# Turning the thresholded weights: TensorE takes row tiles 1 and 3 of the first eight head pairs, and the instruction order is planned anew

## The chip, the cores and the metric

The kernel runs on one core of one Trainium2 chip. The metric is the device time of the whole kernel in microseconds. Before the change it is 623.7 us, the median of three runs (623.29 to 623.73). The profiled run took 623.28 us, of which the profile covers a span of 621.5 us from the first to the last instruction, so a span and a time of this kernel differ by 1.8 to 2.2 us.

## What is computed

```python
scores = (q @ k.T) / 8                       # 8 batches, 8 heads, 576 x 576, head size 64
thresh = scores.max(-1) - tau                # tau = 0.02
attn   = exp(where(scores >= thresh, scores, -1e9) - scores.max(-1))
x      = (attn / (attn.sum(-1) + 1e-9)) @ v  # heads side by side: 8 x 576 x 512
u      = x + (x.T @ U @ V).T                 # rank 32, along the sequence
out    = u + relu(u @ w_ch1) @ w_ch2         # 512 -> 2048 -> 512
```

## The kernel before

**Pairs and row tiles.** The work is cut into 32 pairs of heads, four pairs to a batch. A pair's 576 rows are nine half tiles of 64, handled as row tiles 0 to 3 of 128 rows and a tile 4 that two neighbouring pairs share. So two pairs make nine score blocks, and the kernel has 144 of them. I number the blocks from 0, in the order in which TensorE runs them. Batch 0 is blocks 0 to 17, batch 1 blocks 18 to 35.

**One score block.** TensorE writes the scores of both heads into two PSUM tiles (`scores`, L449). VectorE reads each of them once, scaled and negated, to SBUF and takes the row minimum on the way (`weigh`, L462). There is one such pair of PSUM tiles only, so block n+1 can't start before both reads of block n are done. ScalarE makes the threshold (L475) and the exponentials (L482). VectorE selects and sums (`select`, L489) into a bf16 tile of the ring `w_ring`, which holds four blocks.

**Turning.** The product with `v` (`product`, L582, for the first four pairs L586) contracts over the columns, so the selected weights have to be turned. There are two ways. `turn_w` (L502) is a DMA transpose that SyncE issues, for one head or for both at once. `turn_pe` (L509) is five TensorE transposes into a PSUM bank, after which ScalarE copies the bank to SBUF (`copy_w`, L519). Before the change, the first eight pairs (`EARLY = 8`) turn row tiles 1, 2 and 3 of head 1 on TensorE and of head 0 by one-head transfers; row tile 0 and the shared tile go by two-head transfers. Head 0 of row tile 3 of pair 3 goes to TensorE too. All later pairs use two-head transfers only.

**What follows a pair.** The products are scaled by the inverse sums (`make`, L607, or for later pairs `low_part`, `join`, `norm`), then come `narrow` (L635), the low-rank products `low_rank` (L643) and `spread` (L658, and `spread4`, L695, once a batch), the sum `sum_u` (L665), `narrow_u` (L672) and a turn by TensorE, `turn_u` (L680), copied by `copy_u` (L686). When all four pairs of a batch are through, the mixer of that batch may run: 16 `up` groups of four matmuls (L750) with a relu on ScalarE each (L740), and `down` groups of four (L783), four to an output tile. The row tile 4 of two batches is done together: `rest` (L766).

**The order.** A planner in the kernel, the class `Order`, decides the order of every engine's instructions when the kernel is built. It holds a list of tasks with a cost and dependencies, keeps a clock for each engine, and takes from the tasks that can start within `PATIENCE` of the earliest the one with the lowest rank, which is the time when it became ready plus an offset by kind and phase from the table `OFF`. Mixer tasks have a due step, counted in score blocks (`DUE`); before it they are taken only when nothing else can start. Where the planner sees TensorE idle it puts filler matmuls on a zero tile (`fill`, L293). [...]

**Buffers that matter below.** Four PSUM banks for all that isn't scores, two `wT_ring` buffers for the turned weights (pair p needs the products of pair p-2 to be done), two `qkraw` buffers, and GpSimd's queue for the loads of q, k and the mixer's weights (`W1_AT` and `W2_AT` name the block whose read opens each weight load).

## Time and profile before

| | busy us | share of the 621.5 us span |
|---|---|---|
| TensorE matmul | 604.8 | 97% |
| VectorE | 521.5 | 84% |
| ScalarE | 479.3 | 77% |
| GpSimd | 285.5 | 46% |

A matmul is recorded from its start until its modelled end, so records of neighbours overlap. The spacing from one start to the next is what a matmul costs. The page's second part cuts the span into 40 slices of 15.5 us and prints the busy share of each in tenths. The timeline lists instructions in order of time, with equal neighbours merged into one row: start, length, engine, line, operation, tiles, count, and, in brackets, how long the engine was idle before and what ended that.

The program has 73 fillers and 25 turns by TensorE (125 matmuls of L509). The span has 127 DMA transposes into `wT_ring` and 16 into `wT4`.

### The profile page before, as it was taken

The page shows a single profiled execution, that of the slowest core. Times are in us where ns is not written, and L with a number is a line of the kernel's source. Part 1 is how long each engine was busy: PE and PEld are TensorE (multiplying, and loading weights), DVE is VectorE, ACT ScalarE, POOL GpSimd, SP SyncE. Part 2 cuts the span into 40 slices and gives each one's busy share as a digit, 9 for nine tenths or more (in the row PEclk, how much of TensorE's full clock was granted, in tenths as well). Part 3 has the DMA queues.
Part 4 walks back from the last instruction along what each step waited for, and adds up shares of the span by engine and source line. Part 5 has one row for each costly group of instructions (what it writes and reads, how often), then busy time and mean ns, then how long its engine had stood idle before and what let it go on. Part 6 is the DMA issues. An engine that isn't in the chain of part 4 may idle for free.

```text
span 621.5 us, 16829 instructions
## 1 busy us (share of the span) xinstructions
PE 604.8 (97%) x6286; PEld 353.2 (57%) x6374; DVE 521.5 (84%) x1406; ACT 479.3 (77%) x983; POOL 285.5 (46%) x396
## 2 busy tenths in 40 slices
PE   8989999999999999999999999999999999999996
PEld 4556555565665655555656555555656555555543
DVE  5999998799888999899988999899999898993202
ACT  5779899978898767987898976897798867893540
POOL 8965456545455544535455554444565513211000
PEclk9999999999999999999999999999999999999999
DMA  7999999876976988889979898989998676653303
GB/s 161 172 169 175 154 141 170 137 134 129 171 141 121 169 156 163 140 145 167 161 142 148 135 163 151 150 134 177 162 135 170 141 124 118 117 93 60 69 1 84
DMA packets 205105, 86.27 MB, mean 139 GB/s; under 512 B 183136, under 2 KB 195376, under 8 KB 205024
## 3 DMA queue, kind: packets, MB, share of 16 engines
q1 hardware_dynamic: 190096, 62.23, 62.2%
q0 software_dynamic: 14048, 22.76, 18.7%
q8 instruction: 50, 0.82, 0.6%
q10 hardware_dynamic: 880, 0.21, 0.2%
q14 instruction: 31, 0.25, 0.2%
HBM read 36.86 MB, written 9.44 MB: 74 GB/s over the span
## 4 chain that ended last, share of the span: by engine, by line
PE 85%; DVE 8%; issue 3%; ACT 1%; DMA 1%; SPq 1%; DVEq 0%; ACTq 0%
PE scores L449 23%; PE bank L783 20%; PE bank L750 17%; PE bank L582 12%; PE bank L383 4%; DVE w_ring L489 3%; DVE s_sb L462 3%; PE bank L766 2%; PE bank L643 1%; PE bank L658 1%; PE bank L680 1%; PE bank L396 1%; DMA vraw_ring<-in_v_dram 1%; PE bank L509 1%; ACT e_sb L482 1%
## 5 line engine op out<-in xcount | busy, mean ns | idle before, releaser
L489 DVE SCALAR_TENSOR_TENSOR w_ring<-s_sb,thr,e_sb 128x576 bf16<-128x576 f32 x288 | 238.4, 846 | 10.2 <-ACT thr L475 5.2
L482 ACT ACTIVATE e_sb<-s_sb,m 128x576 bf16<-128x576 f32 x288 | 217.2, 770 | 27.2 <-DVE s_sb L462 26.1
L462 DVE TENSOR_SCALAR_CACHE_REDUCE s_sb<-scores 128x576 f32<-128x576 f32 x288 | 207.9, 751 | 30.9 <-PE scores L449 27.6
L449 PE MATMUL scores<-qkT 64*64 64x288 f32 x2304 | 178.8, 415 | 1.1 <-DVE s_sb L462 1.0
L630 POOL TENSOR_TENSOR x<-x,rec 128x256 f32<-128x256 f32 (+1 forms) x84 | 58.9, 702 | 169.3 <-DVE x L623 108.2
L783 PE MATMUL bank<-W2b,R 128*128 128x512 bf16 x541 | 133.3, 379 | 2.4 <-issue 0.6
L750 PE MATMUL bank<-uT,W1b 128*128 128x512 bf16 x470 | 120.0, 379 | 2.5 <-issue 0.5
L449 PEld LDWEIGHTS scores<-qkT 64*64 64x64 f32 x2304 | 78.0, 132 | 74.6 <-issue 17.8
L740 ACT ACTIVATE R<-bank 128x512 bf16<-128x512 f32 x144 | 84.5, 594 | 22.4 <-PE bank L750 14.5
L329 POOL DMA_DIRECT2D qkraw<-in_q_dram x125 | 81.9, 661 | 33.2 <-PE bank L383 26.9
L415 POOL TENSOR_TENSOR vh<-vraw_ring,vh 128x640 bf16<-128x640 f32 x32 | 50.6, 1581 | 78.8 <-ACT vh L411 69.2
L783 PEld LDWEIGHTS <-R 128*128 128x128 bf16 x576 | 53.3, 98 | 56.3 <-issue 5.7
L329 POOL DMA_DIRECT2D qkraw<-in_k_dram x125 | 81.2, 656 | 3.8 <-DMA qkraw<-in_q_dram 2.3
L750 PEld LDWEIGHTS <-W1b 128*128 128x128 bf16 x512 | 46.0, 98 | 52.1 <-issue 10.2
L582 PEld LDWEIGHTS <-wT_ring 128*128 128x128 bf16 x1120 | 64.8, 98 | 12.7 <-issue 8.8
L582 PE MATMUL bank<-vh,wT_ring 128*128 128x128 bf16 x1120 | 71.9, 219 | 0.0
L794 DVE TENSOR_TENSOR o<-bank,x 128x512 f32<-128x512 f32 x36 | 24.4, 683 | 39.7 <-PE bank L783 36.7
L475 ACT ACTIVATE thr<-m,tau_t 128x2 f32<-128x2 f32 x144 | 42.2, 293 | 4.6 <-DVE s_sb L462 4.2
L389 ACT COPY qkT<-bank 128x512 f32<-128x512 f32 x64 | 35.5, 584 | 9.5 <-PE bank L383 9.1
L623 DVE TENSOR_TENSOR x<-bank,x 128x256 f32<-128x256 f32 (+1 forms) x84 | 30.7, 375 | 8.1 <-ACT x L619 7.3
L383 PE MATMUL bank<-ident,qkraw 128*128 128x128 f32 x256 | 34.9, 275 | 1.0 <-DMA qkraw<-in_q_dram 0.3
L619 ACT COPY x<-bank 128x256 f32<-128x256 f32 (+1 forms) x84 | 26.7, 329 | 10.6 <-PE bank L582 9.9
(70 smaller groups left out, 498.2 us busy)
## 6 DMA issues: line engine op xcount, KB each, us to landing
out_dram<-o SPq DMA_DIRECT2D x72, 128.0 KB, 2.5
vraw_ring<-in_v_dram SPq DMA_DIRECT2D x32, 160.0 KB, 3.7
qkraw<-in_k_dram POOLq DMA_DIRECT2D x63, 80.0 KB, 4.8
qkraw<-in_q_dram POOLq DMA_DIRECT2D x62, 80.0 KB, 3.9
vraw_ring<-in_v_dram SPq DMA_DIRECT2D x32, 128.0 KB, 4.3
qkraw<-in_q_dram POOLq DMA_DIRECT2D x63, 64.0 KB, 4.1
qkraw<-in_k_dram POOLq DMA_DIRECT2D x62, 64.0 KB, 4.4
W1b<-in_moe_w_ch_dram POOLq DMA_DIRECT2D x8, 256.0 KB, 5.5
```

What stands on the lines that cost most here:

```text
L329: queue.dma_start(pr.qkraw[part, to, j, :], src[:, j, of, :])
L383: nc.tensor.transpose(bank[t.got[0]][:, i * P:(i + 1) * P], pr.qkraw[:, t0 + i, :, :], ident)
L415: nc.gpsimd.tensor_tensor(out=pr.vh[:, :, :, 1, :], in0=pr.vraw.rearrange("p j t d -> p t j d"), in1=pr.vh[:, :, :, 0, :], op=ALU.subtract)
L449: nc.tensor.matmul(pair_bank[j][part, c, 0:HC], a.tT[hs, 0, rows], a.tT[hs, 1, cs], start=True, stop=True)
L462: nc.vector.tensor_scalar(out=s_sb.rearrange("p (a c) -> p a c", a=2), in0=pair_bank[x][:, :, 0:HC], scalar1=-scale, scalar2=None, op0=ALU ...
L482: nc.scalar.activation(out=e_sb, in_=s_sb, func=ACT.Exp, bias=m[:, x:x + 1], scale=-1.0)
L489: nc.vector.scalar_tensor_tensor(out=w_sb[:, 0:S], in0=s_sb, scalar=thr_[:, x:x + 1], in1=e_sb, op0=ALU.is_le, op1=ALU.mult, accum_out=pr. ...
L582: nc.tensor.matmul(av[:, 2 * a + j, :], w, pr.vh[:, kt, j, :, :], start=first, stop=last_)
L630: nc.gpsimd.tensor_tensor(out=x, in0=x, in1=over_sum(part), op=ALU.mult)
L740: nc.scalar.activation(out=R2[:, fts, lo:hi], in_=bank[t.got[0]].rearrange("p (f c) -> p f c", c=hi - lo), func=ACT.Relu)
L750: nc.tensor.matmul(bank[t.got[0]], W1b[:, dt, ft * P:(ft + 1) * P], bt.uT[:, dt, :], start=(dt == 0), stop=(dt == 3))
L783: nc.tensor.matmul(ch, R2[:, ft, lo:lo + P], W2b[:, ft, :], start=(ft == 0), stop=(ft == 15))
```

## The change

In the first eight pairs, row tiles 1 and 3 of both heads are now turned by TensorE, and row tiles 0 and 2 by one transfer for both heads. This leaves no one-head transfer: 23 of them go, 8 two-head transfers and 7 turns by TensorE are added. At the same time the planner gets new numbers: the offsets `OFF`, the patience of GpSimd and SyncE, the landing times of transfers, the issue cost of a two-head transpose (1.9 to 1.4), and the due steps of weights and mixers. Two dependencies are added for the planner: a product waits until the output rows that it leads to are free (`opens`), and the first `down` of a tile waits for the one of the tile before (`got("down")`). What is computed stays the same. It is meant to relieve the DMA queue in the crowded opening and to fit the order to that.

```diff
-BOTH = 1.9
-W1_AT = (5, 7, 9, 11, 13, 15, 17, 19)
-W2_AT = (21, 22, 24, 25, 26, 27, 29, 30)
-DUE = (30, 48, 99, 104, 159, 168, 132, 156)
+W1_AT = (0, 3, 6, 8, 11, 14, 17, 19)
+W2_AT = (20, 21, 23, 24, 25, 26, 28, 29)
+DUE = (30, 48, 66, 84, 162, 120, 128, 156)
...
-    PATIENCE = (0, 0.2, 0.1, 0.55, 0)
+    PATIENCE = (0, 0.2, 0.1, 1.1, 1.35)
...
-    LANDING = (2.3, 1.8)
+    LANDING = (2.0, 1.4)
...
-        "down": (0, 0, 0), "exponential": (21, 43, -10.5), "finish": (-2, -4, -1),
+        "down": (0, 0, 0), "exponential": (27.75, 43, -10.5), "finish": (-2, 13, -1),
...
-        "turn_pe": (-25, 13, -1), "turn_rest": (-3, -2, -2), "turn_u": (-23, -6, -3),
+        "turn_pe": (-20.25, 13, -1), "turn_rest": (-5, -37.25, -6.25), "turn_u": (-36, -6, -3),
...
-            both = not (p < EARLY and 1 <= i < 4)
+            both = not (p < EARLY and i in (1, 3))
...
-            if i < 4 and (x == 1 and p < EARLY and i >= 1 or p == NPAIR - 1 and i == 3):
+            if i < 4 and (p < EARLY and i in (1, 3)):
...
-                    SP, BOTH, turn_w, [first_sel, sel] + free, dma=2.2)
+                    SP, 1.4, turn_w, [first_sel, sel] + free, dma=2.2)
...
-                done["wTs", p, g] + [done["vlo", p], got("AV", p - 1, g)], banks=1, kind="AV")
+                done["wTs", p, g] + [done["vlo", p], got("AV", p - 1, g)] + opens, banks=1, kind="AV")
...
-                    when=due + 38.75 * ft / 16)
+                    when=due + 35.75 * ft / 16)
...
-                        kind="p1", when=due + -11.75 + 9.75 * g)
+                        kind="p1", when=due + -0.75 + 10 * g)
...
-                when = due + 124 if i == 4 and b < B - 1 else due + 20.5 + 0.25 * (i + g / 4) / 4
-                halves.append(add(PE, 0.865, down, (relus4 if i == 4 else relus) + weights2 + halves,
-                                  banks=int(not g), kind="ch", when=when))
+                when = due + 133.5 if i == 4 and b < B - 1 else due + 48.5 + 14.25 * (i + g / 4) / 4
+                halves.append(add(PE, 0.865, down, (relus4 if i == 4 else relus) + weights2 + (
+                    halves or [got("down")]), banks=int(not g), kind="ch", when=when))
+            done["down"] = halves[0]
```

## The prediction

> **What bounds the kernel now.** I read the page's second part first, then the windows by stage, then the timelines of TensorE and VectorE around the stage borders.

> ```profile
> PE   8989999999999999999999999999999999999996
> DVE  5999998799888999899988999899999898993202
> ACT  5779899978898767987898976897798867893540
> ```

> TensorE looks full nearly everywhere, but its record has overlapping ends, so I don't trust the digit. The windows show a difference of stage.

> ```profile
> 12.00:83.00 71.00, 65.79 (x942) 40.55 (x941) 69.64 (x188) 57.48 (x115) 47.28 (x70) 1.00 1.13 163
> 83.00:91.00 8.00, 7.95 (x92) 5.39 (x88) 7.75 (x22) 7.02 (x15) 4.53 (x7) 1.00 1.17 210
> 91.00:557.00 466.00, 461.32 (x4825) 270.91 (x4896) 424.88 (x1146) 387.33 (x805) 220.43 (x297) 1.00 0.84 145
> 557.00:617.00 60.00, 59.40 (x387) 31.61 (x390) 14.04 (x31) 22.45 (x43) 3.21 (x5) 1.00 0.26 54
> ```

> The columns are window, length, busy time of TensorE matmuls, weight loads, VectorE, ScalarE and GpSimd, then clock, DMA share, GB/s. From 12 to 83 us VectorE is busy for 69.64 of 71 us: it is the bound, and TensorE has room (67 of the 73 fillers lie before block 23). From 91 us on VectorE has about 9% to spare and TensorE none.

> To find the border I added up the TensorE work in program order at the spacing that the timeline shows between starts: 1.13 us for a score block and 0.095 us for entering it, 0.863 for four `up` or `down` matmuls, 1.12 for twenty products (1.16 in the first four pairs), 0.87 for the eight turns of q and k and 0.14 for the ninth, 0.285 for a turn of weights, 0.28, 0.235 and 0.225 for `low_rank`, `spread` and `turn_u`, 0.056 for a matmul of `rest`, 0.216 for a filler or `spread4`. The clock minus this sum is lost time. It is 3.8 us at the end of block 0, 9.3 at block 12, 16.34 at block 22 (end 83.13 us), 17.29 at block 24 (90.77 us), 17.44 at block 25, and then hardly grows: 19.56 at block 143 (557.05 us). So from block 24 to the end TensorE runs without a gap, and everything that it holds is time. The border:

> ```profile
> 82.00 1.69 PE L449 MATMUL scores<-qkT 64*64 64x288 f32 x16
> ...
> 85.63 1.49 PE L449 MATMUL scores<-qkT 64*64 64x288 f32 x16
> 87.06 0.40 PE L680 MATMUL bank<-identb,ub 128*128 128x128 bf16 x4
> 87.29 1.28 PE L582 MATMUL bank<-vh,wT_ring 128*128 128x128 bf16 x20
> 88.41 1.03 PE L750 MATMUL bank<-uT,W1b 128*128 128x512 bf16 x3
> ```

> The block at 82.00 is number 22; the first `up` comes after block 23. The last 64 `down` start at 602.79 us, end at about 616.6, and the last addition and store take the remaining 4.9 us.

> [...] the records here do overlap, hence the sum over spacings. [...] the select is stuck behind the subtraction of GpSimd that began just before it and takes 1.93 us where 0.8 is usual.

> ```profile
> 36.95 1.40 POOL L415 TENSOR_TENSOR vh<-vraw_ring,vh 128x640 bf16<-128x640 f32 x1 [3.04 <-ACT vh L411]
> 37.04 1.93 DVE L489 SCALAR_TENSOR_TENSOR w_ring<-s_sb,thr,e_sb 128x576 bf16<-128x576 f32 x1
> ```

> **The change part by part.** *Turns on TensorE.* 7 x 5 = 35 matmuls are added. In the changed program 20 of them (90 against 70) come before the end of block 22, where TensorE is not the bound: no cost, hidden behind VectorE. The other 15 (70 against 55) are three turns on the path: 3 x 0.285 = 0.86 us.

> *Fillers.* 67 instead of 73, but 57 instead of 67 before block 22 ends and 10 instead of 6 after it: 4 x 0.216 = 0.86 us more on the path. (The ten: one ahead of block 23, six ahead of 31, three ahead of 42, none before the last `down`, where the old order has three.)

> *Work moved ahead of the border.* One `spread` (0.235) and one `spread4` (0.216) now come before block 22: 0.45 us less after it. The counts of all other TensorE work after block 22 are equal. So after block 22 the new order has 0.86 + 0.86 - 0.45 = 1.27 us more.

> *An earlier border.* The first `up` moves from after block 23 to before it. Between the ends of blocks 22 and 23 the new order holds 4.66 us of TensorE work, the old one 2.97 (with 3.63 on the clock). So TensorE is the bound from block 22 on instead of 24, and the 17.29 - 16.34 = 0.95 us that the old order loses between those blocks is gone. Net: +0.3 us for the same date of block 22.

> *The date of block 22.* It is VectorE's. Up to the two reads of block 21, which release block 22, both VectorE lists hold exactly the same instructions (the sums at 0.68 a read, 0.74 a select are equal), so the date moves only by stalls. Downward: of the 71 us, 1.4 are idle and some 3 us are selects stretched by GpSimd (1.93 and 1.83 us twice, 1.28, 1.20, 1.19); at best 2 us of this goes. Upward: ScalarE. Seven copies at 0.58 us spacing (0.69 as recorded) are 4.1 us more, and they fall here: at the exponentials of block 22 its list holds 68.7 us instead of 63.4, at a spacing of 0.68 an exponential. From block 10 to 21 it holds 36.7 us against 36.6 of VectorE work; before, it was 32.4. ScalarE becomes a second bound there, with no more than VectorE's own stalls to spare. I take +0.2 us, bounds -2 and +2.5.

> *The chain into the first `up`.* Between `low_rank` and `spread` of pair 3 the old order has two turns and the score matmuls of block 22, 1.6 us, the new one only one turn of 0.285 us, in which ScalarE's copy (0.26 us as recorded, plus two signals and its queue) can't fit. Likewise between `turn_u` and `up` there is 0.65 us (four turns of q or k and a filler) instead of 1.12 us of products, for a copy of 0.58 us. What waits behind these on TensorE is block 23 and all after it. The trace has no such wait; the nearest, products behind a copy at 35.28 us, idled 0.66 us. I take 0.3 us, bounds 0 and 1.5.

> *DMA.* 23 one-head transfers go and 8 two-head ones come: 15 issues fewer, at 1.2 to 1.4 us of SyncE each. No TensorE time after block 24 waits for a transfer now, so nothing is gained after the border; before it VectorE hides it. Products still come 2 to 3 blocks or more after their last select (1.5 in a few cases, all with a last tile turned by TensorE), so I cost this at nothing.

> *The steady part and the end.* New due steps change which mixer work fills a block, not how much there is. The new `opens` holds back the products of batch 7: pairs 28 and 29 run after block 139 instead of 131 to 138. Nine transposes then follow in a row; the last product has about 28 us of TensorE work between, enough for nine at 2.4 us (the spacing of four in 9.80 us at 553 us). I take 0, upper bound 2 us. The last group and the 4.9 us after it are alike.

> Sum: 0.3 + 0.2 + 0.3 = +0.8 us: 623.7 + 0.8 = 624.5 us.

> **Rivals.**
> *Slower: ScalarE and the tight chains.* The 4.1 us on ScalarE hold up selects before block 22, waits in front of `spread` and `up` open, the batched transposes make the end late. For it: 36.7 against 36.6 us[...]. Against it: ScalarE is busy only 57.48 of the 71 us now. With half of each upper bound (1.2 + 0.8 + 1.0) less the 0.5 already taken: about +2.5 on 624.5, so 627.0 us.
> *Faster: fewer collisions.* GpSimd's subtractions and casts fall between selects, VectorE starts block 22 up to 2 us earlier and the chains hold. 623.7 + 0.3 - 2.0 = 622.0 us. For it: five stretched selects. Against it: there are as many subtractions as before, and where they fall is chance. The transposes by DMA can't be the gain, since nothing on the path waits for them.
> *No change because the copies are hidden* is the forecast itself.

> **How the numbers follow.** Forecast, near no change: 0.42, 624.5 us. Slower rival: 0.36, 627.0. Faster rival: 0.22, 622.0. 0.2% is 1.25 us, so no change is 622.45 to 624.95. The forecast lies near its upper edge, so 0.05 of it goes to slower. Faster 0.22, same 0.37, slower 0.41. Range: from the faster rival less 1 us for gains that I don't see, 621.0, up to 623.7 + 0.3 + two thirds of the upper bounds of 2.5, 1.5 and 2 us, 628.0.

> **What would show it.** Right: 32 turns and 67 fillers, block 22 still ending near 83 us, VectorE full up to it, TensorE without a gap from block 22 on, and the rest from there as long as before within a microsecond. ScalarE as bound: idle time of L489 behind L482 before 83 us. The chains: idle time ahead of L658 or L750 near 85 us. The end: idle TensorE near 560 us. It is wrong if the lost time after block 24 grows by more than 2 us or block 22 moves by more than 2 us.

## The result and the profile after

The changed kernel takes 632.7 us, the median of four runs (631.9 to 634.0). Its ratio to the kernel before is 1.0135, with a 95% interval of 1.0096 to 1.0174: some 8 to 9 us slower. A ratio here is an estimate over the executions and not the quotient of the two medians, and it leaves out executions that are over 1.5% above the fastest of their kernel. The profiled execution took 634.0 us with a span of 632.2 us, so it shows 10.7 us more than the span of before; I account for that one.

The second part of the page:

```profile
PE   8889899999999999999999999999999999999997
DVE  5989998799998899899997999899998899785101
ACT  5669789988799867897889876897788865596530
PEclk9989899999999999999999999999999999999999
```

TensorE's granted clock falls twice in the first five slices; in the kernel before this row is 9 throughout. The windows by stage, cut where the same work ends in the new trace (block 22, the border, block 143), with the columns as before:

```profile
12.00:88.30 76.30, 69.11 (x968) 43.20 (x963) 70.07 (x189) 59.55 (x119) 48.64 (x70) 0.96 0.94 150
88.30:97.40 9.10, 9.10 (x96) 5.53 (x92) 7.70 (x20) 8.80 (x19) 6.80 (x10) 1.00 0.81 163
97.40:567.30 469.90, 467.34 (x4886) 270.01 (x4882) 424.99 (x1141) 384.62 (x798) 220.91 (x293) 1.00 0.82 142
567.30:628.00 60.70, 60.23 (x419) 32.52 (x411) 16.42 (x36) 26.23 (x51) 3.21 (x6) 1.00 0.28 53
```

The opening is 5.3 us longer up to block 22, but VectorE's busy time in it hardly grew (70.07 us against 69.64): VectorE now waits for 6 us there. The clock minus the sum of TensorE work, the measure of the prediction, shows where the 10.7 us lie. (All times in the table are counted from the first score block at the same date; the prices are those of the prediction to within 0.2 us in the sum.)

| up to the end of | before, us | lost | after, us | lost |
|---|---|---|---|---|
| block 6 | 27.2 | 5.0 | 27.9 | 6.4 |
| block 8 | 33.7 | 6.1 | 38.1 | 10.7 |
| block 15 | 56.9 | 11.4 | 60.4 | 15.4 |
| block 17 | 64.3 | 12.3 | 71.0 | 19.8 |
| block 22 | 83.3 | 16.5 | 88.6 | 22.4 |
| block 37 | 142.8 | 17.4 | 150.1 | 22.5 |
| block 42 | 161.4 | 17.5 | 171.7 | 25.3 |
| block 120 | 466.3 | 18.9 | 471.8 | 26.8 |
| block 121 | 470.8 | 18.8 | 476.7 | 28.6 |
| block 143 | 556.7 | 19.2 | 567.5 | 29.4 |

So the new order loses 5.9 us more up to block 22. After it it loses 7.0 us where the old one loses 2.7, in pieces: 2.8 between blocks 37 and 42, 1.8 at block 121, 0.6 each near blocks 82 and 132. From block 143 on both take the same time. In the opening, the view of TensorE's waits (columns: who waited for whom, us in total, times, longest) names two long ones. First after, from 10 to 90 us:

```profile
PE bank L585 <- DMA wT_ring<-w_ring: 2.3, 1, 2.3
PE scores L448 <- DVE s_sb L461: 2.2, 1, 2.2
PE bank L679 <- ACT wT_ring L518: 0.9, 1, 0.9
```

The same view of before has no wait over 0.7 us and none for a transposing transfer:

```profile
PE bank L509 <- DVE w_ring L489: 1.3, 3, 0.6
PE scores L449 <- DVE s_sb L462: 1.0, 2, 0.7
PE bank L586 <- ACT wT_ring L519: 0.7, 1, 0.7
```

**The first wait.** TensorE's timeline of after (lines of kernel.py are one lower than before):

```profile
28.06 0.66 PE L382 MATMUL bank<-ident,qkraw 128*128 128x128 f32 x4
31.05 1.34 PE L585 MATMUL bank<-vh,wT_ring 128*128 128x64 bf16 x40 [2.33 <-DMA wT_ring<-w_ring]
32.22 0.31 PE L395 MATMUL bank<-ident,qkraw 128*128 128x128 f32 x1
32.46 2.16 PE L448 MATMUL scores<-qkT 64*64 64x288 f32 x16
34.55 1.11 PE L382 MATMUL bank<-ident,qkraw 128*128 128x128 f32 x4
```

The product of pair 0, row tiles 2 and 3, waits for the two-head transfer of row tile 2. The view of its tile from 20 to 26 us has that one transfer, issued at 22.0 us, and its landing, 9.0 us after the issue:

```profile
L501 SPq DMA_TRANSPOSE wT_ring<-w_ring x1: 2009/2009/2009, 22.0 to 22.0; - x1
DMA to landing us min/median/max: 9.0/9.0/9.0
```

The scores of block 7 (the expectations below call it block 8), queued behind it, then take 2.16 us where 1.2 is usual, and four turns 1.11 instead of 0.66. The windows cut at the trace's own clock records say why: the window with the wait in it has only 1.51 us of TensorE, and the next 3.41 us run at half the clock.

```profile
29.15:32.56 3.41, 1.51 (x45) 1.40 (x49) 1.62 (x7) 1.12 (x3) 2.13 (x4) 1.00 0.96 160
32.56:35.97 3.41, 3.41 (x22) 1.76 (x23) 2.36 (x6) 1.21 (x3) 2.74 (x5) 0.50 1.28 149
```

**The second wait.** The full timeline of after, a collision of VectorE's select and GpSimd's subtraction:

```profile
61.52 2.48 DVE L488 SCALAR_TENSOR_TENSOR w_ring<-s_sb,thr,e_sb 128x576 bf16<-128x576 f32 x1
...
61.97 1.41 POOL L414 TENSOR_TENSOR vh<-vraw_ring,vh 128x640 bf16<-128x640 f32 x1
...
64.14 0.76 DVE L461 TENSOR_SCALAR_CACHE_REDUCE s_sb<-scores 128x576 f32<-128x576 f32 x1
...
64.96 0.47 PE L448 MATMUL scores<-qkT 64*64 64x288 f32 x4 [2.21 <-DVE s_sb L461]
```

The select is recorded from 61.52 us, before the subtraction, but ends only 0.6 us after it. The dates alone don't show that it waited for the subtraction; e9 below, which cuts only that, does (0.92 us instead of 2.48). The read of block 15 behind it is late, block 16 waits 2.21 us, and again 3.41 us of half clock follow:

```profile
63.28:66.69 3.41, 1.73 (x15) 0.80 (x16) 2.96 (x9) 1.75 (x4) 0.60 (x2) 1.00 0.61 90
66.69:70.10 3.41, 3.41 (x47) 2.69 (x49) 2.99 (x9) 2.51 (x5) 0.00 (x0) 0.50 0.82 160
```

### The profile page after: what moved, and what is told of

The parts are those of the page before. It is cut to its first block, busy times and chain, and to the rows that moved or that the text cites. A ratio compares the mean times of both kernels' runs of the same rounds, so it can differ in the third digit from the quotient of the medians.

```text
span 632.2 us, 16962 instructions
## 1 busy us (share of the span) xinstructions
PE 615.1 (97%) x6403; PEld 355.6 (56%) x6403; DVE 524.1 (83%) x1406; ACT 483.8 (77%) x990; POOL 289.1 (46%) x396
## 4 chain that ended last, share of the span: by engine, by line
PE 85%; DVE 5%; DMA 4%; ACT 2%; issue 2%; POOL 1%; SPq 1%; DVEq 0%; POOLq 0%; ACTq 0%
PE scores L448 22%; PE bank L782 19%; PE bank L749 17%; PE bank L581 12%; PE bank L382 4%; DMA wT_ring<-w_ring 3%; DVE w_ring L488 2%; PE bank L765 2%; DVE s_sb L461 2%; PE bank L642 1%; DMA vraw_ring<-in_v_dram 1%; PE bank L679 1%; PE bank L395 1%; PE bank L585 1%; PE bank L657 1%
## 5 line engine op out<-in xcount | busy, mean ns | idle before, releaser
L481 ACT ACTIVATE e_sb<-s_sb,m 128x576 bf16<-128x576 f32 x288 | 217.2, 770 | 38.0 <-DVE s_sb L461 37.3
L448 PE MATMUL scores<-qkT 64*64 64x288 f32 x2304 | 181.4, 417 | 2.4 <-DVE s_sb L461 2.4
L629 POOL TENSOR_TENSOR x<-x,rec 128x256 f32<-128x256 f32 (+1 forms) x84 | 61.2, 730 | 166.7 <-DVE x L622 113.3
L782 PE MATMUL bank<-W2b,R 128*128 128x512 bf16 x576 | 137.4, 379 | 0.0
L749 PE MATMUL bank<-uT,W1b 128*128 128x512 bf16 x512 | 123.7, 379 | 0.0
L739 ACT ACTIVATE R<-bank 128x512 bf16<-128x512 f32 x144 | 85.1, 595 | 20.8 <-PE bank L749 16.5
L581 PEld LDWEIGHTS <-wT_ring 128*128 128x128 bf16 x1120 | 64.0, 98 | 14.8 <-issue 11.4
L388 ACT COPY qkT<-bank 128x512 f32<-128x512 f32 x64 | 35.6, 584 | 10.2 <-PE bank L382 10.0
L382 PEld LDWEIGHTS bank<-ident,qkraw 128*128 128x128 f32 x256 | 29.4, 142 | 5.3 <-issue 2.5
```

The costliest lines, as they stand in the source:

```text
L382: nc.tensor.transpose(bank[t.got[0]][:, i * P:(i + 1) * P], pr.qkraw[:, t0 + i, :, :], ident)
L448: nc.tensor.matmul(pair_bank[j][part, c, 0:HC], a.tT[hs, 0, rows], a.tT[hs, 1, cs], start=True, stop=True)
L481: nc.scalar.activation(out=e_sb, in_=s_sb, func=ACT.Exp, bias=m[:, x:x + 1], scale=-1.0)
L581: nc.tensor.matmul(av[:, 2 * a + j, :], w, pr.vh[:, kt, j, :, :], start=first, stop=last_)
L629: nc.gpsimd.tensor_tensor(out=x, in0=x, in1=over_sum(part), op=ALU.mult)
L739: nc.scalar.activation(out=R2[:, fts, lo:hi], in_=bank[t.got[0]].rearrange("p (f c) -> p f c", c=hi - lo), func=ACT.Relu)
```

## The experiments

The ratios below are to the kernel before, run on the same chip, with 95% intervals. "The order kept" means that the planner's list is written down before anything is emitted (`plan`) and only the named entries of it are moved or added; numbers are positions of tasks in the list.

| run | median us | ratio |
|---|---|---|
| changed kernel | 632.7 | 1.0135 [1.0096, 1.0174] |
| e1 turning rule alone | 632.2 | 1.0130 [1.0086, 1.0174] |
| e2 new numbers alone | 631.9 | 1.0131 [1.0108, 1.0153] |
| e8 old kernel, one landing time moved 3% | 632.1 | 1.0123 [1.0079, 1.0167] |
| e3 nine fillers in the wait | 630.6 | 1.0108 [1.0087, 1.0128] |
| e4 product later | 630.6 | 1.0108 [1.0085, 1.0131] |
| e5 weights later | 629.2 | 1.0086 [1.0061, 1.0111] |
| e9 subtraction cut in five | 628.2 | 1.0067 [1.0044, 1.0089] |
| e18 weights later and cut | 625.6 | 1.0030 [1.0008, 1.0052] |
| e11 weights later, cut, nine fillers | 629.2 | 1.0083 [1.0051, 1.0115] |
| e16 changed, 19 fillers more | 632.0 | 1.0141 [1.0121, 1.0160] |
| e6 changed, no subtraction | 623.9 | 0.9997 [0.9966, 1.0028] |
| e7 before, no subtraction | 619.9 | 0.9944 [0.9922, 0.9966] |
| e12 e8 without subtraction | 623.5 | 0.9989 [0.9969, 1.0010] |
| e10 before, cut | 628.0 | 1.0051 [1.0025, 1.0076] |
| e13 before, 35 fillers fewer | 623.7 | 1.0012 [0.9987, 1.0037] |
| e14 before, 18 fillers more | 623.6 | 1.0032 [0.9993, 1.0072] |
| e15 before, cut, 18 fillers more | 631.3 | 1.0125 [1.0090, 1.0160] |
| e17 before, cut, weights later | 632.8 | 1.0115 [1.0054, 1.0177] |

### Which half of the change costs the time: e1, e2, e8

e1 is the kernel before with the new turning rule and `opens`, e2 the changed kernel with the old rule, e8 the kernel before with `opens` and a number that means nothing.

```diff
 # e1, on before; e2 is the reverse, on after
-            both = not (p < EARLY and 1 <= i < 4)
+            both = not (p < EARLY and i in (1, 3))
-            if i < 4 and (x == 1 and p < EARLY and i >= 1 or p == NPAIR - 1 and i == 3):
+            if i < 4 and (p < EARLY and i in (1, 3)):
 # e8, on before
-    LANDING = (2.3, 1.8)
+    LANDING = (2.3, 1.85)
```

> The kernel before with the new turning rule and the dependency `opens` only (with the old ranks the planner finds no order for the rule without `opens`); ranks, due steps, weight loads, patience and landing times stay old. If the rule itself costs the time (a two-head transfer can start only when both heads are selected, so a product waits longer for it): about 629 to 633 us, with a product waiting for a transfer near 30 us. If the new ranks and load order cost it: within 2 us of 623.7, and no wait of over 1 us for a transfer in the first 80 us. If ScalarE's seven more copies cost it: 626 to 628 us, with selects idle behind exponentials between 60 and 80 us.

> The changed kernel with the old turning rule (row tiles 1, 2 and 3 of head 1 on TensorE, head 0 by one-head transfers); everything else as changed. If the new ranks and the weight loads ahead of the q and k loads cost the time: still 629 to 634 us. If the turning rule costs it: 622 to 625 us. ScalarE theory: 625 us or less, as the seven copies are gone.

> The kernel before with one number of the planner moved by 3% (landing time of SyncE's transfers 1.8 to 1.85 us) and `opens`, which alone leaves the order as it was. Turning rule, ranks and load order are the old ones; the order is the same up to about 110 us and another one after. If any newly planned order loses what the new one loses after block 24 (5 us), the old one being a lucky one: 626 to 629 us. If the loss comes from the new ranks and due steps themselves: 623 to 625 us.

Each half alone costs the 8 us that both cost together, so they don't add up, and e8 costs as much with neither, more than the 629 us that I had allowed it. e1 by its expectation speaks for the turning rule, e2 for the numbers; e8 takes the force from both: an order planned anew for no reason can take 632 us as well. It is one such order, so it doesn't show that every new order would. They don't lose the time at one place. e1's waits from 10 to 90 us:

```profile
PE bank L586 <- DMA wT_ring<-w_ring: 5.4, 3, 3.0
PE bank L658 <- ACT tt L649: 1.0, 2, 0.7
PE bank L383 <- ACT wT_ring L519: 0.7, 1, 0.7
```

With the same seven more copies on ScalarE as the changed kernel, e1 waits 5.4 us for two-head transfers and never over 0.7 us for ScalarE: the ScalarE rival falls. Its two long waits are 2.98 us at 47.5 us and 2.04 us at 79.3 us, not near 30 us as expected, for transfers that landed 9.7 and 7.9 us after their issue. e2's long wait is a score block for VectorE, and both reach block 22 with 21.0 and 20.6 us lost. e8 has the old opening (17.3 us lost at block 24) and loses 6.8 us between blocks 24 and 143, where the kernel before loses 2.1 and the changed one 7.0; its last 68 us lose another 1.9. No window of half clock stands in its trace before the last score block, and its four executions had a granted clock of 0.997 to 1.000, so e8 loses its time without the clock.

### The late transfer and the half clock: e3, e4, e5

Three edits on the changed kernel, the order kept: fill the wait, put the product elsewhere, or make the transfer early.

```diff
+        plan[at(121):at(121)] = [(PE, 1, None)] * 9          # e3: fillers ahead of the product
+        after(121, 136); after(132, 145)                     # e4: product behind a turn of k, its scaling later
+        for n, m in ((34, 185), (83, 231), (124, 248)):      # e5: three weight loads later
+            after(n, m)
```

> The changed kernel's order with nine fillers more (9 x 0.216 = 1.94 us) just ahead of the product that waits 2.33 us for the transfer of row tile 2. They fit into the wait. If the half clock that follows (block 8's sixteen score matmuls took 2.16 us instead of 1.2, the turns after it 1.11 instead of 0.66) is set off by the idle TensorE: the clock stays full at 32 to 36 us, block 8 ends about 1.2 us sooner and the time is about 631.5 us. If the half clock has another cause: nothing changes, 632.7 us. If VectorE's wait alone counts: 632.7 us as well, with a full clock.

> The changed kernel's order with the product of pair 0, row tiles 2 and 3, one block later on TensorE, and VectorE's scaling of it two instructions later; no transfer is touched. If the wait of this product (2.33 us) and the half clock after it hold up block 8 and so VectorE: block 8 ends 3 to 3.5 us sooner, and the time falls to about 629.5 us. If the transfers themselves are late for all that follows, the wait only moves to the next product: 632 us or more.

> The changed kernel's order; only the first three loads of mixer weights (256 KB each, issued at 11.1, 20.2 and 26.6 us) are moved behind the loads of q and k in GpSimd's queue, to after 40 us. If these loads make the transfer of row tile 2 late (it landed 9.0 us after its issue): it lands 2 us or more sooner, the wait of its product falls from 2.33 us to below 0.5 us, the clock stays full, about 629.5 us. If the transfer is late because it carries two heads and is issued after the second select: the wait stays near 2 us, 632 us.

In e3 the wait is filled, the clock stays full (1.00 from 28.8 to 35.6 us), and the scores behind the product take their usual time. TensorE's timeline:

```profile
28.87 2.11 PE L308 MATMUL bank<-idle 128*128 128x512 bf16 x9
30.81 1.33 PE L601 MATMUL bank<-vh,wT_ring 128*128 128x64 bf16 x40
31.98 0.31 PE L411 MATMUL bank<-ident,qkraw 128*128 128x128 f32 x1
32.22 1.20 PE L464 MATMUL scores<-qkT 64*64 64x288 f32 x16
```

Counted from the first score block, the product comes 0.7 us sooner and block 8 ends 2.3 us sooner: in this pair of executions about 1.6 us of the first loss were the half clock, not the wait. Later in e3 the long collision stayed away too (no select takes over 1.5 us before 88 us), so its median isn't the price of the clock. In e4 the wait is moved out of VectorE's way; block 8 ends 2.2 us sooner (expected were 3 to 3.5) and the clock stays full there, but the collision at block 16 comes back with its half clock. Both gave 2.2 us in the median. In e5 the three loads were issued at 32.1, 37.3 and 37.8 us, behind the transfer in question though not after 40 us as the expectation has it. The transfer lands 6.2 us after its issue, the product has no wait, and block 8 ends 3.9 us sooner. The landing, in the view of the tile from 20 to 26 us, and TensorE's timeline:

```profile
DMA to landing us min/median/max: 6.2/6.2/6.2
```

```profile
27.94 0.66 PE L399 MATMUL bank<-ident,qkraw 128*128 128x128 f32 x4
28.44 1.33 PE L602 MATMUL bank<-vh,wT_ring 128*128 128x64 bf16 x40
29.60 0.30 PE L412 MATMUL bank<-ident,qkraw 128*128 128x128 f32 x1
29.84 1.37 PE L465 MATMUL scores<-qkT 64*64 64x288 f32 x16
```

So the new steps of the weight loads (`W1_AT`) are one cause of the late transfer: with the loads moved it landed after 6.2 us, 6.3 (e18) and 6.6 (e11). Not the only one: with the loads left where the change put them it landed after 9.0, 8.0 (e3), 7.7 (e4), 8.2 (e16) and 7.2 us (e9, where the product waited only 0.53 us). In e5 the collision at block 16 also stayed away, as everything came some 3 us sooner; the 3.6 us that e5 gains are both.

### Does idle time set the clock: e13, e14, e16

If so, fillers everywhere should protect the clock, and taking them out should cost it.

```diff
 # e13: entries without a task (fillers) are left out between score blocks 3 and 22
 # e14 (before) and e16 (after): one more behind the score blocks from 3 to 21
+            if t is not None and t.kind == "S":
+                blocks += 1
+                due = 3 < blocks < 23
+            elif t is not None and c[0] == PE and t.got and due:
+                out.append((PE, t.got[0], None))
+                due = False
```

> The kernel before in its own order without the 35 fillers between score blocks 3 and 22; nothing else changes. TensorE isn't the bound there. If a TensorE that idles too much of a stretch of 3.4 us gets half the clock for the next 3.4 us: several windows of half clock before 85 us and 3 to 12 us more, 627 to 635 us. If the half clock in the other runs has another cause than idle time: 623.5 us and a full clock.

> The kernel before in its own order with 18 fillers more (3.9 us of TensorE work, one after each score block from 3 to 20, in a bank that the next work takes anyway). If its clock is full all the time and VectorE sets the pace: 623.5 to 624.5 us, a little more where a filler delays the work behind it, and less spread between executions. If its pace suffers from TensorE work: 627 us.

> The changed kernel in its own order with 18 fillers more, one after each score block from 3 to 20. If idle TensorE and the half clock after it are what makes stalls in the opening dear: no window of half clock, 629 to 631 us (the collisions and the steady part remain). If the stalls cost by themselves: 632 to 633 us.

None of the three came out as a whole. In e13, without 35 of its fillers the kernel before takes the same 623.7 us in the median, but its clock suffers: nine of the 12 executions of e13 had a granted clock of 0.986 to 0.996, where 21 of the 23 of the kernel before on that chip had 0.998 or more. Five of these nine, at 0.993 to 0.996, took 622.9 to 624.1 us all the same, so in them the lower clock cost no time; where it fell in those five no trace shows. Eighteen fillers more don't protect it: seven executions of e14 took 622.5 to 623.7 us at 0.998 or more, five 628.6 to 631.3 at 0.994 to 0.996. e16, whose edit adds 19 fillers and not 18, takes 632.0 us in the median, as expected if the stalls cost by themselves, and its profiled execution, without a window of half clock, took 631.0. In the profiled executions of e13 and e14 the clock fell after waits of 3.7 and 5.3 us for a transfer, and in e13 at 33 us without any such wait.

To see what goes before a fall I cut all 20 traces at the grid of their clock records, 3.41 us, and summed the time without a TensorE record in each window, from 4 us to 560 us after the start. Fourteen windows at full clock are followed by one at half: thirteen of them hold 1.58 to 3.40 us of idle time, one (e13 at 30 us) 0.97. Of the 3,205 other windows at full clock only three hold more than 1.4 us (1.45, 1.50 and 1.71). So in these traces the clock mostly fell after a window with 1.58 us or more of idle time out of 3.41, which one long wait or two neighbours gave; the border isn't sharp, and the 0.97 stands outside it. The two half windows of after start 34.13 us apart, ten windows of the grid, and the windows ahead of them hold 1.90 and 1.68 us of idle time, so a window that was idle for about half was enough. When the full clock comes back is less clear: of the four windows at half clock that are followed by a second, two hold only 0.25 and 0.57 us of idle time.

### The collisions: e6, e7, e9, e12

e6 (changed), e7 (before) and e12 (e8) write zeros in place of the low half of `v`, so that part is missing from their products; e9 keeps it and cuts the subtraction.

```diff
-            nc.gpsimd.tensor_tensor(out=pr.vh[:, :, :, 1, :], ..., op=ALU.subtract)
+            nc.gpsimd.memset(pr.vh[:, :, :, 1, :], 0.0)          # e6, e7, e12
 # e9
+            for t in range(NT):
+                nc.gpsimd.tensor_tensor(out=pr.vh[:, t, :, 1, :], in0=pr.vraw[:, :, t, :],
+                                        in1=pr.vh[:, t, :, 0, :], op=ALU.subtract)
```

> The changed kernel without the subtraction that makes the low half of v: GpSimd writes zeros in its place, so the low half is left out of the products; the instruction order is the same. It takes away what holds up selects (2.48 us at 61.5 us, 1.95 at 149.0, 1.82 at 157.3). If these hold up the kernel: block 16's wait of 2.21 us and the half clock after it go (about 3 us), the chain at 150 to 170 us gains up to 1 us more: 628.5 us. If the collisions only fall on VectorE's slack: 632 us.

> The kernel before with the same edit (zeros in place of the low half of v). Its selects are stretched too (1.93 us at 36.9, 1.83 at 69.5, 2.06 at 398 us), but no TensorE wait of over 1 us follows. If collisions cost both orders alike: 1.5 to 3 us less, near 621.5 us. If they cost time only where the clock falls after them: within 1 us of 623.8 us.

> The kernel before, planned anew with the landing time of 1.85 us, and zeros in place of the low half of v (left out of the products). If what a new order loses (8.6 us) is that its subtractions and selects meet at bad places: 620 to 623 us, near the 619.9 us of the old order without subtractions. If it loses by its own waits and by work left over at the end: 627 us or more.

> The changed kernel with the subtraction of v's low half cut into five instructions of 128x128 on GpSimd; nothing is left out and every other engine's order is the same. If the loss comes from selects that wait for one whole subtraction (1.4 us): none waits longer than about 0.4 us, block 16's wait and the half clock after it go, and most of the 8.8 us that the kernel without subtractions gained comes back: 625 to 628 us. If five short collisions cost as much as a long one: 631 us or more.

Without subtractions the changed kernel gains 8.8 us, e8 8.6 and the kernel before 3.6; the first and the last are more than I expected. That is the largest effect of the study, and it isn't that the new order has more collisions: from 0 to 88 us its selects take 3.2 us more than 0.81 us each, those of before 3.3. It is where they fall, and what follows. The edit also does more than take away the collisions: the memset takes 0.65 us where the subtraction takes 1.4, so GpSimd issues its loads sooner, and e6 has no first wait either. So the 8.8 us are not all collisions. Nor do the subtractions explain the whole loss: with neither kernel doing any, the new order still takes 4.0 us more (623.9 against 619.9), and their profiled executions reach the end of block 22 within 0.4 us.

e9 is the cleaner test. In the place of block 16's collision it shows (GpSimd, then VectorE):

```profile
60.87 2.30 POOL L415 TENSOR_TENSOR vh<-vraw_ring,vh 128x128 bf16<-128x128 f32 x5
```

```profile
60.42 0.92 DVE L488 SCALAR_TENSOR_TENSOR w_ring<-s_sb,thr,e_sb 128x576 bf16<-128x576 f32 x1
```

The select meets the subtraction at the same place and takes 0.92 us instead of 2.48; block 16 waits 0.65 us instead of 2.21, and no half clock follows. From 45 us to 560 us no select takes over 1.2 us. At this place the shorter subtractions (0.46 us each) held the select up less than the whole one of 1.41 us. In the traces of before and after every select of over 1.2 us, 8 and 9 of 288, overlaps a subtraction, while of the reads of scores that overlap one (34 and 33) none took over 0.76 us. Two selects of e9, near 12 and 40 us, still took 1.89 and 1.96 us. e9 gains 4.6 us.

### Both repairs, and the kernel before: e18, e11, e10, e15, e17

> The changed kernel in its own order with the cut subtraction and its first three weight loads after 40 us. Alone the two gave 628.2 and 629.2 us. If they remove different losses (the collisions, and the late transfer with the half clock after it): 626 us. If they remove the same one, the half clock after the wait: 628 us.

> The changed kernel's order with three edits together: the first three weight loads after 40 us, nine fillers ahead of the product of row tiles 2 and 3, and the cut subtraction. If the opening's loss is the late transfer, the half clock and the collisions: block 22 ends within 1 us of the kernel before (83.3 us; 88.6 in the changed kernel), and 624 to 626.5 us remain, the rest of the loss being steady. If the new order is slow in itself: 628 us or more.

e18 puts e5 and e9 together (the three loads now at 33.0 to 40.4 us): 625.6 us, as expected if they remove different losses. Its waits from 10 to 84 us:

```profile
PE scores L465 <- DVE s_sb L478: 1.1, 2, 0.7
PE bank L602 <- DMA wT_ring<-w_ring: 0.9, 1, 0.9
PE bank L696 <- ACT wT_ring L535: 0.7, 1, 0.7
```

Block 22 ends at 82.9 us, 0.4 us sooner than before, with a full clock. What is left of the loss against before is after it: 16.7 us lost at block 22, 20.6 at block 143. That the new turning and the new order cost the opening nothing doesn't follow, since the cut helps both kernels there: in the profiled execution of e10, the kernel before with the same cut, block 22 ends at 80.9 us, 2.0 us sooner than in e18. Without subtractions the two orders are 0.4 us apart (81.1 us in e7, 81.5 in e6). e11, the same as e18 with e3's nine fillers, is slower (629.2 us): its block 22 ends 4.3 us later than that of e18, and in its profile a window of half clock came at 68 us. That the fillers, with the transfer early, only push work back is my reading; no run shows it.

> The kernel before with the same cut. Without subtractions it gained 3.6 us. If the cut frees most of that: 621 to 622.5 us, faster than both kernels. If not: 623.5 us or more.

> The kernel before with the cut subtraction (which gave 622.0 to 633.5 us at granted clocks of 1.000 to 0.988) and the same 18 fillers. If the spread comes from windows of half clock after idle TensorE, the fillers close it: clock at 0.998 or more and about 622.5 us, faster than both kernels. If the cut itself is slow: 627 us again.

> The kernel before in its own order with the cut subtraction, and three loads of mixer weights (issued at 50.2, 57.1 and 61.1 us) moved behind GpSimd's subtraction at 69.4 us. With the cut alone it took 622.0 to 633.5 us, and in executions of the same order with fillers products waited up to 5.3 us at 60 to 66 us for transfers that landed 9 to 14 us after their issue instead of 4 to 8.5. If the DMA engines are what runs short there: landings below 8.5 us, clock at 0.998 or more, 621 to 622.5 us with little spread. If not: 627 us with the same spread.

The same cut doesn't help the kernel before. Its 20 executions run from 622.0 to 633.5 us, and loosely by granted clock: 622.6 to 624.2 at 1.000, 632.7 and 633.5 at 0.990 and 0.988, but also 631.2 at 0.997. The one that was profiled took 622.7 us, so no trace shows a late one. e15 and e17 missed both of their expectations. Their profiles and e14's show what is late there. TensorE in e14:

```profile
66.24 1.25 PE L603 MATMUL bank<-vh,wT_ring 128*128 128x64 bf16 x20 [5.32 <-DMA wT_ring<-w_ring]
```

The transfers into `wT_ring` that were issued from about 44 to 68 us landed (minimum, median, maximum, us after the issue), in before and then in e14:

```profile
DMA to landing us min/median/max: 4.4/6.4/8.5
```

```profile
DMA to landing us min/median/max: 8.9/11.1/13.8
```

With the same transfers in the same order, and 18 fillers more, they take 9 to 14 us in one execution where they take 4 to 8.5 in the other; TensorE then waits up to 5.3 us and loses the clock on top (0.56 of it granted from 63.6 to 67.1 us, 0.50 from 67.1 to 70.5). Of the profiled executions that keep the old order but for such edits, the four over 628 us (e13, e14, e15, e17) all have transfers there that landed after about 12 us or more, and the three under 624 us (before, e7, e10) have none over 10.0. In the changed kernel the transfers issued from 40 to 70 us landed after

```profile
DMA to landing us min/median/max: 3.8/4.7/5.6
```

So in these traces the change does relieve the DMA queue, as it was meant to, but from 40 us on, where the old order mostly got by. And it owes this to its numbers more than to its turning: from 40 to 70 us the transfers landed after 2.6 to 6.3 us in e2 (new numbers, old turning) and after 6.2 to 8.8 us in e1 (new turning, old numbers). Why the transfers are late in those executions I can't say: in e17 no weight load was issued between 49 and 79 us, and the transposes issued from 50 to 62 us still landed after 9.1 to 12.0 us. No kernel here that computes everything beats the one before in the median.

## Why the prediction was wrong

I forecast 624.5 us, within 621.0 to 628.0; it is 632.7. The step that failed first is the date of block 22, with the DMA in front of it costed at nothing; the steady part failed second.

**The date of block 22: wrong, and the largest miss.** The step took +0.2 us with bounds of -2 and +2.5; measured is +5.3. The bounds were built from VectorE's own stalls, counted only as something to win, and ScalarE's copies. The upper one didn't hold: what came was a 2.33 us wait for a transfer and a 2.48 us collision, and each was followed by 3.41 us of half clock. e3 shows that the clock was worth about 1.6 us at the first place, and in e18, with both causes removed, block 22 ends at 82.9 us, within 0.6 us of the step's figure. Since the cut moves block 22 in the kernel before too, the fairer pair is e6 and e7, without subtractions: 0.4 us apart, where the step has 0.2. So the base of the step held, and what its bounds lacked was a late transfer, a stretched select right ahead of a score block, and the clock after either.

**DMA costed at nothing: wrong.** I wrote that VectorE hides transfers before the border and that products come two to three blocks after their last select. The second is true of the new order as well (the select of row tile 2 ended near 22 us, the product was due at 28.7), and it isn't enough, as a transfer took 9.0 us where the slack was 6.7. I had counted the issues (15 fewer) and not the landings, and I passed over `W1_AT`, which puts three loads of 256 KB into the first 27 us where there was one. In e5, with those loads later, the transfer took 6.2 us and the wait was gone.

**ScalarE as the slower rival: wrong cause.** The outcome was on the slower side, but e1 with the same copies waits at most 0.7 us for ScalarE, and in after the only listed wait of a select before 88 us is 1.4 us for the first threshold, at 12 us (0.8 before).

**Turns, fillers and the border: right.** TensorE's work by the same sum is 0.7 us more in all. From block 22 on it runs without a gap, as forecast: 22.4 us lost there and 22.4 at block 24, where before lost 0.6 between them (16.5 and 17.1). No listed wait stands ahead of the `spread` at 86.6 us or the first `up` at 90.2 us: the tight chains cost nothing, inside their bounds of 0 to 1.5.

**The steady part: wrong in size.** I took 0 with an upper bound of 2 us; the profiled execution loses 7.0 us from block 24 to 143 where before lost 2.1. The argument that due steps only move work was sound for the amount of work and said nothing of where waits and collisions land. Two selects of 1.95 and 1.82 us at 149 and 157 us precede the loss at blocks 37 to 42, and without subtractions (e6) 1.3 us are lost from block 37 to 42 instead of 2.8. The 1.6 us wait at block 121 is again a product waiting for a transfer, and it is gone in e5, e6, e9 and e18. The waits view lists 2.6 of these microseconds; the rest I haven't traced. Subtractions are part of it and not all: from block 24 to 143 e6 loses 3.9 us and e7, the old order without them, 1.4. That e8 loses 6.8 us there with the old ranks and due steps shows that it doesn't take the new ones to lose it.

**The end: right.** From the last score block on both kernels take the same time, and the nine transposes in a row let nobody wait.

## What to carry to other kernels

## What I had not expected

- Half the clock came mostly after windows with 1.58 us or more of idle time out of 3.41, not after wholly idle ones. In e5, seven executions of one order run from 627.6 us at a granted clock of 1.000 to 630.7 us at 0.994.
- One order of instructions can take 622.0 us in one execution and 633.5 in another: the kernel before with the cut subtraction. Late transposing transfers, as in e15 and e17, are the likely cause; its own late executions have no trace.
- Filler matmuls in a VectorE-bound stretch kept the clock up (0.998 or more in 21 of 23 executions) and were worth nothing in the median time: 623.7 us without 35 of them, at a granted clock down to 0.986.
